# Emitting the next batch's attention in hand-ordered small units inside this batch's FFN, with column-tiled AV, two-bank scores, Silu and 128-token output tiles

## The chip, the cores and the metric

One core of a Trainium2 chip. The metric is the device time of one execution in microseconds (us), lower is better. Each kernel was run several times; runs of one kernel agree within about 1%, all runs quoted here are of the fast state (none lies more than 1.5% above the fastest of its kernel), and each experiment was timed beside the kernel before on the same chip.

Names of engines in the profile: PE is the matrix engine, PEld its weight loads, DVE the vector engine, ACT the scalar (activation) engine, POOL the engine that issues the cast-while-loading DMAs here, SP the one that issues the output DMAs. Both kernels put the sums of their matmuls into tiles of PSUM (the `psum` and `ps_` pools), from which DVE and ACT read them; a bank below is the part of such a tile that holds the scores of one head. The granted clock is the share of its full speed that the profile records for PE.

## The reference

Attention without softmax (squared relu; its second product, attention times V, is called AV below), then a gated FFN with an RMS norm. Eight batches of 448 tokens, 12 heads of 64, model width 768, FFN width 1536.

```python
scores = (1 / sqrt(64)) * q @ k.T                 # per batch and head, 448 x 448
attn   = maximum(scores, 0) ** 2 / 448
x      = concat_heads(attn @ v)                   # 3584 tokens x 768
xn     = x / sqrt(mean(x * x) + 1e-6) * rms_g
out    = (silu(xn @ w_gate) * (xn @ w_val)) @ w_out
```

Everything on PE is bf16 with fp32 sums.

## The kernel before

Tokens of a batch are cut into four chunks of 112 (`PC`). For a pair of heads, Q and K are transposed on PE, scores are computed per chunk and head (64-row matmuls, one PSUM bank each), relu is shared between ACT (head 0) and DVE (head 1), the square is on DVE. AV uses a zero-padded V, 128 columns wide, so that both heads of a pair add into one [128, 448] tile. `xT` is the transposed attention output, which the FFN of the same batch reads.

```python
def attention_pair(b, j, xT, qkv, fillers=()):
    ...                                            # transposes, copies to QT and KT_
    for c in range(NCH):
        for hh in range(2):
            psS = psum.tile([PC, S], FP32, tag=tg, bufs=bf)
            nc.tensor.matmul(out=psS[:], lhsT=KT_[prt, c*PC:(c+1)*PC], rhs=QT[prt, :], ...)
        rA: nc.scalar.activation(Relu, pss[0]);  nc.vector.tensor_tensor(rA * rA)
        rB: nc.vector.tensor_relu(pss[1]);       nc.vector.tensor_tensor(rB * rB)
    if fillers: fillers.pop(0)()                   # a piece of the FFN of batch b-1
    for hh in range(2):
        for c in range(NCH):
            nc.tensor.matmul(out=psAV[:], lhsT=vpad[:, c, hh, :], rhs=rsq[hh][c][:], ...)
    ...
    nc.scalar.mul(out=xT[:, j, :], in_=psAV[:], mul=inv_attn)

def norm():
    x2 = xT * xT                                   # one DVE instruction, 2688 columns
    for kt in range(KT): psSS += ones @ x2[:, kt]  # PE: sum over the model width
    rstdb = Sqrt(psSS / 768 + eps)                 # ACT
    nc.vector.reciprocal(rstdb)                    # DVE
    for kt in range(KT): xn[:, kt] = xT[:, kt] * g * rstdb      # DVE, six instructions

def gate(fb):                                      # 12 of these per batch
    psG = wg.T @ xn (6 matmuls);  psV = wv.T @ xn (6 matmuls)
    sig = Sigmoid(psG)                             # ACT
    t1 = sig * psG;  hT[:, fb, :] = t1 * psV       # DVE, two instructions

def outproj(u):                                    # four tiles of 112 tokens per batch
    for o, w in ((0, 512), (512, 256)):
        12 matmuls: psO += hT[:, fk, u*PC:(u+1)*PC].T @ wo_sb[:, fk, o:o+w]
        nc.vector.tensor_copy(ost[:, o:o+w], psO)

for b in range(NB):                                # FFN of batch b-1 as fillers in attention of b
    work = ffn_chunks(b - 1, ...)                  # [norm, gate x 12, outproj x 4]
    for j in range(HP): attention_pair(b, j, xT, qkvs[j], fillers=3 pieces of work)
ffn_batch(NB - 1, ...)
```

The norm of a batch is the *first* piece of its FFN, so it comes when the attention of that batch has just ended. The tile scheduler is free to reorder instructions.

## Time and profile before

| | before |
|---|---|
| device time, median | 645.35 us (643.21 to 646.93) |
| span of the profiled run | 641.8 us |
| first reciprocal (one per batch, in the norm) | 59.1 us |
| from reciprocal to reciprocal, batches 2 to 6 | 75.1 us each |
| from the last reciprocal to the end | 54.8 us |
| PE / DVE / ACT busy | 90% / 69% / 40% |

The one reciprocal of each batch is a good clock: the table above is the start, the period and the end. (The first period is longer, 83.8 us, and the last shorter, 68.6; the seven together are 527.9.) These lines are from the page of the profile: span, busy time of each engine with its share, then busy tenths in 40 slices of the span for PE and DVE, and the granted PE clock in tenths.

```profile
span 641.8 us, 8357 instructions
...
PE 575.7 (90%) x3120; PEld 292.4 (46%) x3120; DVE 445.1 (69%) x951; ACT 255.4 (40%) x498; POOL 116.4 (18%) x134
...
PE   5465999979999799988999799997999989997997
...
DVE  4745677578776778669775797857786697757452
...
PEclk9855899998999799997999989997999979998999
```

PE is near 9 everywhere after the start, and about every fifth slice has a dip in PE and in the clock. The timeline around one dip (start us, duration us, engine, line, operation; in brackets the idle time before it and what ended it; rows between are left out):

```profile
286.70 1.28 ACT L230 ACT_TABLE_LOAD   x1
...
286.74 0.59 PE L180 MATMUL psS<-QT,KT 64*112 64x448 bf16 x4 [0.30 <-ACT KT L167]
...
287.99 0.63 ACT L230 ACTIVATE rstdb<-psSS,eps_col 128x448 f32<-128x448 f32 x1
...
293.11 2.94 DVE L237 RECIPROCAL rstdb<-rstdb 128x448 f32<-128x448 f32 x1
...
296.22 3.05 DVE L240 SCALAR_TENSOR_TENSOR xn<-xT,g_sb,rstdb 128x448 bf16<-128x448 bf16 x5
...
296.94 0.57 PE L258 MATMUL psG<-xn,wg_sb 128*128 128x448 bf16 x1
```

From the Sqrt at 287.99 to the first gate matmul at 296.94 the FFN has nothing for PE. The reciprocal starts 4.5 us after Sqrt has ended, and DVE fills that time with relu and squares of the next attention. In the meantime PE has only scraps of attention. Two windows around it (from:to and length in us, then us busy and instructions of PE, PEld, DVE, ACT, POOL, then granted clock, DMA share, GB/s):

```profile
288.00:296.00 8.00, 5.70 (x25) 1.92 (x24) 6.91 (x13) 4.09 (x8) 0.00 (x0) 0.72 0.04 17
296.00:304.00 8.00, 7.53 (x32) 3.35 (x33) 7.97 (x18) 4.40 (x9) 1.40 (x2) 0.85 0.23 16
```

The clock is down to 0.72 and 0.85. And three of the costliest groups (line, engine, operation, output and inputs, shapes, count; busy us and mean ns; idle before):

```profile
L258 PE MATMUL psG<-xn,wg_sb 128*128 128x448 bf16 x576 | 151.1, 364 | 11.5 <-DVE xn L240 8.9
...
L291 PE MATMUL psO<-wo_sb,hT 128*112 128x512 bf16 (+1 forms) x768 | 136.2, 327 | 0.0
...
L200 PE MATMUL psAV<-rA,vpad 112*128 112x448 bf16 x192 | 61.0, 382 | 12.4 <-DMA vpad<-in_v_dram 10.0
```

The mean of 364 ns is not the pace of the matmuls, since the records of neighbouring ones overlap. The pace is better read from a dense stretch of the timeline: 12 gate and value matmuls in a row (from 302.55 us) take 2.27 us, 0.189 us each.

### The profile page before, as it was taken

What the parts mean: (1) busy time and instruction counts of PE and PEld (TensorE: products, weight loads), DVE (VectorE), ACT (ScalarE), POOL (GpSimd) and SP (SyncE); (2) the same over time, 40 slices, a digit from 0 to 9 for tenths busy, and PEclk for the clock granted to TensorE, in tenths of its full rate; (3) what the DMA queues carried; (4) which work ended last, traced back from release to release, by engine and by line L of the source; (5) the groups of instructions that cost most, each with busy time, mean ns of one, the idle gap of its engine ahead of it and who ended that gap; (6) DMA issues with size and microseconds to landing.
All of it is one profiled execution on the core that took longest, in us unless ns stands there. A gap on an engine that the chain in (4) does not pass through costs nothing. (4 is left out here: it accounts for less than half of the span.)

```text
span 641.8 us, 8357 instructions
## 1 busy us (share of the span) xinstructions
PE 575.7 (90%) x3120; PEld 292.4 (46%) x3120; DVE 445.1 (69%) x951; ACT 255.4 (40%) x498; POOL 116.4 (18%) x134
## 2 busy tenths in 40 slices
PE   5465999979999799988999799997999989997997
PEld 2121444644446344553445444463445534454455
DVE  4745677578776778669775797857786697757452
ACT  5532545244532544245352445425442354522210
POOL 9442311301014001130013010040001000100000
PEclk9855899998999799997999989997999979998999
DMA  9999922591119611391124912197112311211002
GB/s 74 169 204 188 125 14 16 69 118 13 11 8 117 77 8 9 37 157 8 7 16 61 126 9 15 7 111 83 8 9 37 72 8 9 14 44 43 1 2 86
DMA packets 139016, 35.14 MB, mean 55 GB/s; under 512 B 132320, under 2 KB 133856, under 8 KB 138976
## 3 DMA queue, kind: packets, MB, share of 16 engines
q0 software_dynamic: 134096, 23.60, 49.3%
q1 hardware_dynamic: 4880, 11.02, 5.5%
q8 instruction: 24, 0.39, 0.2%
q14 instruction: 16, 0.13, 0.1%
HBM read 47.19 MB, written 11.01 MB: 91 GB/s over the span
## 5 line engine op out<-in xcount | busy, mean ns | idle before, releaser
L258 PE MATMUL psG<-xn,wg_sb 128*128 128x448 bf16 x576 | 151.1, 364 | 11.5 <-DVE xn L240 8.9
L193 DVE TENSOR_SCALAR rB<-psS 112x448 bf16<-112x448 f32 x192 | 117.3, 616 | 36.6 <-PE psS L180 36.5
L267 PE MATMUL psV<-xn,wv_sb 128*128 128x448 bf16 x576 | 140.8, 360 | 0.8 <-DVE hT L278 0.2
L291 PE MATMUL psO<-wo_sb,hT 128*112 128x512 bf16 (+1 forms) x768 | 136.2, 327 | 0.0
L109 POOL DMA_DIRECT2D vpad<-in_v_dram x48 | 38.8, 809 | 404.7 <-PE psAV L200 156.9
L180 PE MATMUL psS<-QT,KT 64*112 64x448 bf16 x384 | 88.0, 404 | 24.0 <-ACT rA L189 10.8
L189 ACT ACTIVATE rA<-psS 112x448 bf16<-112x448 f32 x192 | 98.1, 542 | 26.4 <-PE psS L180 25.5
L291 PEld LDWEIGHTS <-hT 128*112 128x112 bf16 x768 | 90.4, 130 | 38.5 <-issue 7.0
L275 ACT ACTIVATE sig<-psG 128x448 bf16<-128x448 f32 x96 | 51.5, 543 | 111.2 <-PE psG L258 80.1
L190 DVE TENSOR_TENSOR rA<-rA 112x448 bf16<-112x448 bf16 x192 | 73.2, 381 | 22.0 <-ACT rA L189 21.5
L267 PEld LDWEIGHTS <-wv_sb 128*128 128x128 bf16 x576 | 54.5, 99 | 68.2 <-issue 27.1
L258 PEld LDWEIGHTS <-wg_sb 128*128 128x128 bf16 x576 | 55.1, 100 | 60.4 <-issue 22.4
L194 DVE TENSOR_TENSOR rB<-rB 112x448 bf16<-112x448 bf16 x192 | 73.4, 382 | 0.3
L200 PE MATMUL psAV<-rA,vpad 112*128 112x448 bf16 x192 | 61.0, 382 | 12.4 <-DMA vpad<-in_v_dram 10.0
L298 DVE COPY ost<-psO 112x512 f32<-112x512 f32 x64 | 35.5, 555 | 49.6 <-PE psO L291 49.6
L200 PEld LDWEIGHTS <-vpad 112*128 112x128 bf16 x384 | 36.7, 103 | 59.1 <-issue 26.4
L180 PEld LDWEIGHTS <-KT 64*112 64x112 bf16 x384 | 28.3, 132 | 77.6 <-issue 53.1
L167 ACT COPY QT<-psT 128x448 bf16<-128x448 bf16 x48 | 25.5, 531 | 90.4 <-PE psT L162 90.2
L200 PE MATMUL psAV<-rB,vpad 112*128 112x448 bf16 x192 | 56.7, 395 | 0.0
L209 ACT ACTIVATE xT<-psAV 128x448 bf16<-128x448 f32 x48 | 26.1, 544 | 68.6 <-PE psAV L200 68.6
L110 POOL DMA_DIRECT2D vpad<-in_v_dram x48 | 38.3, 798 | 0.2
L167 ACT COPY KT<-psT 128x448 bf16<-128x448 bf16 x48 | 25.5, 531 | 30.8 <-PE psT L162 30.7
(243 smaller groups left out, 389.3 us busy)
## 6 DMA issues: line engine op xcount, KB each, us to landing
out_dram<-ost SPq DMA_DIRECT2D x32, 336.0 KB, 2.7
vpad<-in_v_dram POOLq DMA_DIRECT2D x96, 56.0 KB, 2.8
qb<-in_q_dram POOLq DMA_DIRECT2D x7, 672.0 KB, 9.3
kb<-in_k_dram POOLq DMA_DIRECT2D x7, 672.0 KB, 12.4
wg_sb<-in_moe_w_gate_dram POOLq DMA_DIRECT2D x1, 2304.0 KB, 18.0
wv_sb<-in_moe_w_val_dram POOLq DMA_DIRECT2D x1, 2304.0 KB, 25.4
wo_sb<-in_moe_w_out_dram POOLq DMA_DIRECT2D x1, 2304.0 KB, 16.2
qp<-in_q_dram POOLq DMA_DIRECT2D x6, 112.0 KB, 5.1
```

The costliest lines, as they stand in the source:

```text
L109: nc.gpsimd.dma_start(out=vpad[:, :, 0, 0:D], in_=v_head_ap(b, 2 * j))
L167: nc.scalar.copy(out=dst[:], in_=psT[:, ti, :])
L180: nc.tensor.matmul(out=psS[:], lhsT=KT_[prt, c * PC : (c + 1) * PC], rhs=QT[prt, :], start=True, stop=True,)
L189: nc.scalar.activation(out=rA[:], in_=pss[0][:], func=ACT.Relu)
L190: nc.vector.tensor_tensor(out=rA[:], in0=rA[:], in1=rA[:], op=ALU.mult)
L193: nc.vector.tensor_relu(out=rB[:], in_=pss[1][:])
L194: nc.vector.tensor_tensor(out=rB[:], in0=rB[:], in1=rB[:], op=ALU.mult)
L200: nc.tensor.matmul(out=psAV[:], lhsT=vpad[:, c, hh, :], rhs=rsq[hh][c][:], start=(hh == 0 and c == 0), stop=(hh == 1 and c == NCH - 1),)
L258: nc.tensor.matmul(out=psG[:], lhsT=wg_sb[:, kt, fb * P : (fb + 1) * P], rhs=xn[:, kt, :], start=(kt == 0), stop=(kt == KT - 1),)
L267: nc.tensor.matmul(out=psV[:], lhsT=wv_sb[:, kt, fb * P : (fb + 1) * P], rhs=xn[:, kt, :], start=(kt == 0), stop=(kt == KT - 1),)
L275: nc.scalar.activation(out=sig[:], in_=psG[:], func=ACT.Sigmoid)
L291: nc.tensor.matmul(out=psO[:, :w], lhsT=hT[:, fk, u * PC : (u + 1) * PC], rhs=wo_sb[:, fk, o : o + w], start=(fk == 0), stop=(fk == FT - 1),)
```

## The change

The intent is to keep PE fed. The kernel declares a manual schedule, so each engine runs instructions in the order in which the program emits them. That order is built by `merge`: gate, value and out-projection units of batch b, with small units of the attention of b+1 spread over the first 90% of them, the norm of b+1 the last of these. In detail: AV writes each head of a pair to its own 64 columns (no zero padding); two heads' scores lie in two neighbouring banks, so relu and square take 896 columns per instruction (three quarters of the relu on ACT); Silu replaces Sigmoid and a multiply; the out-projection works on 128-token tiles over two batches, seven in place of eight; q, k and v are loaded in 512-byte pieces (in the kernel before, most packets of the trace have 128 bytes) and reordered on DVE; weights are loaded in slices. Some copies out of PSUM also change engine: that of the transposed Q and K goes from ACT to DVE, that of the output from DVE to ACT.

```diff
+def merge(main, side, head=0.0, tail=0.0):
+    total = sum(c for c, _ in main)
+    ...
+    for c, f in main:
+        while k < n and done >= total * (head + (1.0 - head - tail) * k / n):
+            out.append(side[k][1]); k += 1
+        out.append(f); done += c
+    ...
+    ctx.enter_context(tc.manual_schedule())
...
-                psS = psum.tile([PC, S], FP32, name="psS", tag=tg, bufs=bf)
+            psS = ps_s.tile([PC, 2, 512], FP32, name="psS", tag="psS")
...
-            nc.scalar.activation(out=rA[:], in_=pss[0][:], func=ACT.Relu)
-            nc.vector.tensor_relu(out=rB[:], in_=pss[1][:])
+            if on_dve:                                   # every fourth
+                nc.vector.tensor_relu(out=r[:], in_=psS[:, :, :S])
+            else:
+                nc.scalar.activation(out=r[:], in_=psS[:, :, :S], func=ACT.Relu)
+            nc.vector.tensor_tensor(out=r[:], in0=r[:], in1=r[:], op=ALU.mult)
...
-                    out=psAV[:],
-                    lhsT=vpad[:, c, hh, :],
+                    out=psAV[hh * D : (hh + 1) * D, :],
+                    lhsT=ld["v", b][:, 2 * j + hh, c * D : (c + 1) * D],
...
-            nc.scalar.activation(out=sig[:], in_=psG[:], func=ACT.Sigmoid)
-            nc.vector.tensor_tensor(out=t1[:], in0=sig[:], in1=psG[:], op=ALU.mult)
+        nc.scalar.activation(out=s[:], in_=psG[:], func=ACT.Silu)
...
+    def attention(b):
+        units = [(0.4, lambda: transposes(b, 0))]
+        for j in range(HP):
+            units.append((0.5, lambda j=j: scores(b, j, (0, 1))))
+            if j + 1 < HP:
+                units.append((0.4, lambda j=j: transposes(b, j + 1)))
+            units.append((0.5, lambda j=j: scores(b, j, (2, 3))))
+            if j:
+                units.append((0.8, lambda j=j: attend(b, j - 1)))
+        units.append((0.8, lambda: attend(b, HP - 1)))
+        return units
...
+    for fn in merge([], attention(0) + [(1.1, lambda: norm(0))]):
+        fn()
+    for b in range(B):
+        if b + 1 < B:
+            side = attention(b + 1) + [(1.1, lambda b=b: norm(b + 1))]
+        ...                                              # loads of batch b + 2
+        for fn in merge(ffn(b), side, 0.0, 0.1):
+            fn()
```

## The prediction

> **What bounds the kernel now.** PE. Page: PE 90% busy, DVE 69%, ACT 40%. The reciprocal of each batch's norm (timeline) marks the period: 142.9, 218.0, 293.1 ... 518.4 us, 75.1 us per batch. The first comes at 59.1 us (PE waits 9.4 us for a vpad DMA); 54.8 us follow the last.
>
> Dense streams run at full speed: 12 gate/value matmuls take 2.27 us (189 ns for 448 columns), 24 out-projection matmuls 3.94 us. Score pairs (64 rows) already run concurrently: four take 0.58 us. PE work per batch at that pace: gate/value 27.2, out-projection 15.8, scores about 8, AV 48 x 0.189 = 9.1, transposes 3, norm 1.3, together 64-65 us. The other 10 us come around the norm: from 286.7 to 296 us PE runs only bits of attention, waiting for Sqrt, reciprocal (2.94 us) and xn (6 x 0.6 us), and the clock drops to 0.72-0.85 (about 3.4 us lost).
>
> **What the change does to PE, per batch (estimates from these durations).**
> - AV in two 64-column tiles: 24 slots of 0.189[...]: 6 us in place of about 10.[...]
> - 128-token tiles: 7 tiles per two batches in place of 8: 13.8 us in place of 15.8.
> - Scores in fours: about 0.61 us x 12 = 7.3. Transposes 3.3, gate/value and norm as before.
> Sum: even batches 57 us, odd 61.
>
> **Norm.** It is now issued with 5.1 us of out-projection behind it. Chain after its sum: Sqrt 0.63, reciprocal 2.94, xn 3.7, then two reorder copies before the next transposes: about 8 us. So PE idles about 3 us at each boundary, some clock loss (1.5 us mean), and about 1.5 us of small waits: period 62 (even), 66 (odd).
>
> **Other engines.** DVE per batch: squares 24 x 0.61 = 14.8, relu 6 x 1.08 = 6.5, psT copy about 4, reorder 3.4, hT 7.4, norm 6.6, x2 2.3: about 45 us, 72% of the period. ACT: relu 18 x 0.92 = 16.6, Silu 6.5, xT 3.3, copies 3.5, norm with two table loads 3.2: 33 us. Neither becomes the limit. Silu saves one DVE multiply (12 x 0.62).
>
> **Start.** Attention of batch 0 runs alone and is DVE-bound: about 6 us per pair, 36 us, beginning near 7 us; first reciprocal near 47 us in place of 59[...].
>
> **Sum.** First matmul of FFN 0 near 51; four even periods of 62 and three odd of 66: 446; clock and start losses 4; last FFN 43 plus 4.5 tail and its bubble: 50. Span about 551; the timed run is 4.5 us above the span (646.3 against 641.8). **Predicted 556 us, 80% range 533 to 592.** Faster by over 2%: 0.97; within 2%: 0.02; slower: 0.01.
>
> **What would show it.** Reciprocals 62-66 us apart; AV pairs starting together (eight matmuls in about 0.75 us); PE idle 2-4 us before each batch's first gate matmul, released by xn or the reorder copies; clock mean above 0.94; first reciprocal at 45-50 us; DVE 65-75%.
>
> **What would make it wrong.** Column tiles not running together (+4.5 us per batch, about +36); the strict order letting ACT or DVE bursts stall PE inside the FFN (+3 us per batch is +21); the boundary gap throttling the clock every time (+2 us each)..

What is cut is marked. In the AV item the 6 us are 24 x 0.189 = 4.5 us plus 1.5 us, and the sums of 57 and 61, 551 and 556 us hold it. Measured afterwards, a group of eight took 0.88 us, 0.12 more than 4 x 0.189. Of the loads the pages show this: the POOL queue moved 23.6 MB before and after, in 134096 and in 40560 packets, whose time was 49.3% and 31.7% of 16 engines' span.

That score pairs run concurrently is seen in the kernel before: four matmuls start at 286.735, .738, .968 and .972 us. The 3.4 us of lost clock are worked out from the two windows above (8 x 0.28 + 8 x 0.15). The 1.5 us of clock and 1.5 us of small waits per period, and the durations of forms that the kernel before does not have, were estimates. Measured in the changed kernel are 0.916 us for a relu of 896 columns on ACT and 1.084 on DVE, 0.625 for a square of 896, 0.620 for the copy of psT and 0.29 for a reorder copy.

## The result and the profile after

| | before | after |
|---|---|---|
| device time, median | 645.35 us | 548.32 us (546.71 to 548.87) |
| ratio | | 0.850 (0.848 to 0.853) |
| span of the profiled run | 641.8 | 544.9 |
| first reciprocal | 59.1 | 43.95 |
| the seven periods together | 527.9 | 447.2 |
| one even / odd period, late in the run | 75.1 / 75.1 | 61.7 / 64.3 |
| last reciprocal to the end | 54.8 | 53.8 |

Even and odd count the batch whose FFN fills the period; an even one has three token tiles, an odd one four.

A ratio is the mean time of one kernel's fast runs over that of the kernel before in the same rounds, so it is not quite the ratio of the medians that are quoted. Of the 96.9 us of span that went away, the periods gave 80.7, the start 15.2 and the end 1.0. The profiled run is the fastest of its four, 1.6 us under the median. The same lines of the page as before:

```profile
span 544.9 us, 7394 instructions
...
PE 485.1 (89%) x3024; PEld 236.1 (43%) x3024; DVE 338.6 (62%) x586; ACT 252.3 (46%) x369; POOL 34.4 (6%) x45
...
PE   3774999879999799888999799987999899989996
...
DVE  3886677467764677566774677656775677745210
...
PEclk9976999979999899999999999999999999999999
```

PE's share has not risen (90% to 89%); its work became less, and its dips are narrower. From the third boundary on the clock stays at full speed. That is a part of the gain too: in the seven periods and the last FFN PE was busy at half clock for 39.3 us before and 9.5 us after. Gate and value matmuls of the changed kernel started 0.373 us apart at half clock (116.0 to 120.1 us) and 0.189 at full, so half of these times was lost, and about 15 us of the gain is clock (an estimate from the clock records of the two traces). The timeline around one boundary, which answers to the one shown of before:

```profile
231.97 0.95 PE L207 MATMUL psAV<-r,vb 112*64 112x448 bf16 x8
...
232.85 2.76 PE L286 MATMUL psO<-wo_sb,hT 128*128 128x512 bf16 x12
...
236.43 1.48 PE L238 MATMUL psSS<-x_1924,ones_bf 128*128 128x448 bf16 x6
...
237.75 5.37 PE L286 MATMUL psO<-wo_sb,hT 128*128 128x256 bf16 x36
...
239.06 2.95 DVE L246 RECIPROCAL rstd<-rstd 128x448 f32<-128x448 f32 x1 [1.55 <-ACT rstd L243]
...
242.05 3.67 DVE L249 SCALAR_TENSOR_TENSOR xn<-xT,g_sb,rstd 128x448 bf16<-128x448 bf16 x6
...
245.63 0.29 DVE L148 COPY qp<-qb 112x512 bf16<-112x512 bf16 x1
...
245.97 0.37 PE L163 MATMUL psT<-ident,qp 112*128 112x112 bf16 x4 [2.85 <-DVE qp L148]
```

The norm's sum on PE (236.43) is followed by 36 out-projection matmuls, which cover Sqrt, the reciprocal and the first part of xn. PE then waits 2.85 us for the reorder copy of the next batch's Q. The first two rows are one AV group: eight matmuls, from 231.97 until the next unit at 232.85, 0.88 us. The same groups as before:

```profile
L260 PE MATMUL psG<-xn,wg_sb 128*128 128x448 bf16 x576 | 129.4, 360 | 1.1 <-DVE xn L249 1.0
...
L286 PE MATMUL psO<-wo_sb,hT 128*128 128x512 bf16 (+1 forms) x672 | 115.2, 326 | 0.0
...
L207 PE MATMUL psAV<-r,vb 112*64 112x448 bf16 x384 | 47.7, 370 | 4.6 <-DVE qkT L169 3.8
```

And what PE itself waited for (total us, times, longest):

```profile
engine line waited for: us in total, times, longest us
PE psT L163 <- DVE qp L148: 29.6, 8, 7.6
PE psS L182 <- ACT r L197: 7.4, 11, 1.0
```

The first of these holds the boundary: eight waits, 29.6 us. The timeline has them as 4.84 us for the very first load, 7.6 us between the first norm and the first FFN, and 2.86 us at six later boundaries. The reorder copy comes last in a chain of Sqrt, reciprocal and xn, so the copy is named but the chain is what is waited for.

### The profile page after: what moved, and what is told of

It is laid out like the page before. It is cut to its first block, busy times and chain, and to the rows that moved or that the text cites. A ratio compares the mean times of both kernels' runs of the same rounds, so it can differ in the third digit from the quotient of the medians.

```text
span 544.9 us, 7394 instructions
## 1 busy us (share of the span) xinstructions
PE 485.1 (89%) x3024; PEld 236.1 (43%) x3024; DVE 338.6 (62%) x586; ACT 252.3 (46%) x369; POOL 34.4 (6%) x45
## 3 DMA queue, kind: packets, MB, share of 16 engines
q0 software_dynamic: 40560, 23.60, 31.7%
## 4 chain that ended last, share of the span: by engine, by line
PE 73%; DVE 14%; ACT 8%; issue 2%; DMA 1%; POOL 0%; ACTq 0%; POOLq 0%
PE psV L260 20%; PE psG L260 20%; PE psO L286 14%; PE psAV L207 8%; PE psS L182 8%; DVE xn L249 5%; DVE rstd L246 4%; ACT r L197 4%; PE psT L163 3%; ACT L243 2%; DVE r L198 2%; DVE r L195 1%; ACT rstd L243 1%; DMA kb<-in_k_dram 1%; ACT xT L215 1%
## 5 line engine op out<-in xcount | busy, mean ns | idle before, releaser
L198 DVE TENSOR_TENSOR r<-r 112x896 bf16<-112x896 bf16 x192 | 119.3, 625 | 93.8 <-ACT r L197 91.9
L197 ACT ACTIVATE r<-psS 112x896 bf16<-112x896 f32 x144 | 127.0, 916 | 52.5 <-PE psS L182 52.4
L286 PE MATMUL psO<-wo_sb,hT 128*128 128x512 bf16 (+1 forms) x672 | 115.2, 326 | 0.0
L271 ACT ACTIVATE sil<-psG 128x448 bf16<-128x448 f32 x96 | 52.3, 545 | 102.2 <-PE psG L260 90.8
L277 DVE TENSOR_TENSOR hT<-sil,psV 128x448 bf16<-128x448 bf16 x96 | 59.4, 618 | 45.9 <-PE psV L260 37.8
L286 PEld LDWEIGHTS <-hT 128*128 128x128 bf16 x672 | 63.6, 98 | 49.2 <-issue 9.3
L182 PE MATMUL psS<-qkT 64*112 64x448 bf16 x384 | 64.5, 394 | 19.3 <-ACT r L197 7.4
L260 PEld LDWEIGHTS <-wg_sb 128*128 128x128 bf16 x576 | 53.0, 99 | 59.8 <-issue 19.2
L260 PEld LDWEIGHTS <-wv_sb 128*128 128x128 bf16 x576 | 52.3, 99 | 57.5 <-issue 19.2
L195 DVE TENSOR_SCALAR r<-psS 112x896 bf16<-112x896 f32 x48 | 52.0, 1084 | 0.0
L207 PE MATMUL psAV<-r,vb 112*64 112x448 bf16 x384 | 47.7, 370 | 4.6 <-DVE qkT L169 3.8
L163 PE MATMUL psT<-ident,qp 112*128 112x112 bf16 x192 | 19.0, 226 | 29.6 <-DVE qp L148 29.6
L207 PEld LDWEIGHTS <-vb 112*64 112x64 bf16 x384 | 19.1, 111 | 28.9 <-issue 21.4
L246 DVE RECIPROCAL rstd<-rstd 128x448 f32<-128x448 f32 x8 | 23.6, 2953 | 12.8 <-ACT rstd L243 12.8
L169 DVE COPY qkT<-psT 128x896 bf16<-128x896 bf16 x48 | 29.8, 620 | 2.3 <-PE psT L163 2.1
```

The costliest lines, as they stand in the source:

```text
L163: nc.tensor.transpose(out=psT[:, ti, c * PC : (c + 1) * PC], in_=ldp[nm, b, j][:, c, :, :], identity=ident[:],)
L182: nc.tensor.matmul(out=psS[:, hh, :S], lhsT=t[prt, 1, c * PC : (c + 1) * PC], rhs=t[prt, 0, :], start=True, stop=True,)
L195: nc.vector.tensor_relu(out=r[:], in_=psS[:, :, :S])
L197: nc.scalar.activation(out=r[:], in_=psS[:, :, :S], func=ACT.Relu)
L198: nc.vector.tensor_tensor(out=r[:], in0=r[:], in1=r[:], op=ALU.mult)
L207: nc.tensor.matmul(out=psAV[hh * D : (hh + 1) * D, :], lhsT=ld["v", b][:, 2 * j + hh, c * D : (c + 1) * D], rhs=rsq[b, j, c][:, hh, :], st ...
```

## The experiments

Two accounts were set against each other. **Theory A**: the periods are the length of PE's own stream plus its waits around the norm; the gain is less PE work (AV, token tiles) and a better covered norm. **Rival B**: the gain came from relieving DVE, whose busy time fell from 445 to 339 us. A third account was not tested by a run: the changed loads. In the first 60 us of the kernel before PE waits 16.2 us for DMAs (vpad 10.0, qp 5.3, kp 0.9), after that only 1.0 us; so the loads may explain much of the 15.2 us at the start, and can explain next to nothing of the later periods. Each experiment starts from the changed kernel unless it says otherwise; differences are to its 548.3 us.

| run | edit | median us | difference |
|---|---|---|---|
| x1_av_serial | AV head by head | 549.4 | +1.1 |
| x2_tiles112 | 112-token tiles | 559.5 | +11.2 |
| x3_norm_last | norm after the FFN | 592.5 | +44.1 |
| x4_sigmoid | Sigmoid and a multiply | 548.5 | +0.2 |
| x8_av_full128 | AV weights 128 wide (wrong result) | 578.1 | +29.8 |
| x9_av_split | heads of a pair apart | 596.0 | +47.7 |
| x5_tail20 | side units over 80% | 526.2 | -22.1 |
| x6_auto | no manual schedule | 511.9 | -36.5 |
| x7_onebank | relu and square per bank | 558.1 | +9.8 |
| y1_auto_tail20 | x6 and x5 together | 507.0 | -41.3 |
| y2_auto_startact | x6, first relus all on ACT | 512.2 | -36.1 |
| b2_coltile | kernel before with column-tiled AV only | 644.1 | -1.3 to before |

The changed kernel was not run again in these batches; the kernel before was, with medians of 644.77, 645.52 and 645.37 us in the three batches, beside 645.35 in the first runs.

### x4_sigmoid: does DVE time count?

```diff
-        nc.scalar.activation(out=s[:], in_=psG[:], func=ACT.Silu)
-        sil[b, fb] = s
+        nc.scalar.activation(out=s[:], in_=psG[:], func=ACT.Sigmoid)
+        nc.vector.tensor_tensor(out=t1[:], in0=s[:], in1=psG[:], op=ALU.mult)
+        sil[b, fb] = t1
```

> The changed kernel with Sigmoid and the extra DVE multiply of before (96 of 0.62 us, 60 us of DVE work, 62% to about 72% of the span). Theory A: 0 to +6 us. Rival B: +35 to +60 us.

Measured: 548.5 us, ratio 0.851 (0.849 to 0.853). The engine line of its page:

```profile
PE 487.4 (89%) x3024; PEld 237.0 (43%) x3024; DVE 390.4 (71%) x682; ACT 252.4 (46%) x369; POOL 34.4 (6%) x45
```

DVE works 390.4 us in place of 338.6 and nothing gets slower. Rival B falls, as far as it is about the sum of DVE's work; the added work stands inside the FFN, so the 4.5 us by which the kernel before kept its reciprocal waiting are not tested here. Silu is a free tidy-up in this kernel and no measurable part of the gain.

### x2_tiles112: the token tiles

```diff
-        for t in range(full) if b % 2 == 0 else range(full, NT):
+        for t in range((b % 2) * NCH, (b % 2) * NCH + NCH):
-   lhsT=hTs[i][:, fk, t * P : (t + 1) * P]
+   lhsT=hTs[i][:, fk, t * PC : (t + 1) * PC]      # copies and stores cut to 112 in the same way
```

> The changed kernel with 112-token out-projection tiles, four in each batch, as before the change. Theory A: one tile (3.9 us of PE) more in each of the four even batches, +15.7 us, less about 1.4 us per even period where two score groups now stand back to back and the fourth tile would part them: +10 to +16 us. Rival B: under +4 us.

Measured: 559.5 us, +11.2, ratio 0.868 (0.865 to 0.871). The seven periods grew from 447.2 to 457.8 us, and the even ones now are as long as the odd ones (64.4 us late in the run). Inside the range of theory A.

### x3_norm_last: where the norm stands

```diff
-            side = attention(b + 1) + [(1.1, lambda b=b: norm(b + 1))]
+            side = attention(b + 1) + [(0.0, lambda: None)]
         for fn in merge(ffn(b), side, 0.0, 0.1):
             fn()
+        if b + 1 < B:
+            norm(b + 1)
```

> The changed kernel, but the norm of the next batch is issued after the last out-projection unit and not with three units (5.1 us) behind it; nothing else moves. Theory A: PE's wait at each of seven boundaries grows from 2.9 to about 8 us, and the granted clock drops each time (2 to 3 us more): +45 to +60 us. Rival B: DVE's work and order hardly change, under +20 us.

Measured: 592.5 us, +44.1, a hair below the range; ratio 0.919 (0.917 to 0.921). Of PE's waits:

```profile
PE psT L163 <- DVE qp L148: 61.5, 8, 8.2
```

Without the two at the start (4.9 and 7.6 us) these are six waits of 8.2 us in place of 2.86, and at every boundary one window of 8 us has a clock of only 0.64 to 0.69. Late periods are 68.8 and 71.1 us in place of 61.7 and 64.3: 7 us each, of which 5.3 are the wait; the rest, about 1.7, is put down to the clock (an estimate by subtraction). Of the parts that were undone here, the position of the norm costs the most.

### x1_av_serial, x8_av_full128, x9_av_split: the column tiles

The first try to take the tiles apart was to swap the loops:

```diff
-        for c in range(NCH):
-            for hh in range(2):
+        for hh in range(2):
+            for c in range(NCH):
```

> The changed kernel, but the AV loop runs head by head, so that two neighbouring matmuls always use the same 64 columns of the array[...]; work, data and result stay the same. Theory A (the periods are the length of PE's own stream): 24 more slots of 0.189 us per batch, 4.5 us in each of the seven full periods, little at the start where DVE sets the pace: +30 to +34 us, about 580 us, ratio to before about 0.90. Rival B (the gain came from relieving DVE, busy 339 us in place of 445; PE has slack): under +8 us.

That matmuls of one head would not overlap was the assumption; x9 below measured 0.88 us for four of them.

Measured: 549.4 us, +1.1, ratio 0.851 (0.845 to 0.856): no effect. Taken alone this looks like evidence against the column tiles. The trace says otherwise; one AV group and the unit after it:

```profile
233.24 0.96 PE L207 MATMUL psAV<-r,vb 112*64 112x448 bf16 x8
234.13 2.76 PE L286 MATMUL psO<-wo_sb,hT 128*128 128x512 bf16 x12
```

Eight matmuls still take 0.89 us, and their records start in pairs 13 to 14 ns apart, 0.19 to 0.21 us from pair to pair. The experiment had not removed what it meant to remove. Two further runs did. The first makes the weights 128 columns wide, with numbers that are wrong on purpose:

```diff
-                    out=psAV[hh * D : (hh + 1) * D, :],
-                    lhsT=ld["v", b][:, 2 * j + hh, c * D : (c + 1) * D],
+                    out=psAV[:],
+                    lhsT=ld["v", b][:, 2 * j + hh, min(c, 2) * D : (min(c, 2) + 2) * D],   # start and stop to match
```

> Wrong result on purpose. The changed kernel with AV weights 128 columns wide (two neighbouring chunks of one head, so the numbers are wrong), eight matmuls into one accumulation, as many and as wide as before the change; nothing else moves. The run before this one (head by head) did not slow down, and its trace shows pairs still starting together. If column tiles are still what made AV shorter, each group of eight takes 8 x 0.189 and not 4 x 0.189 us, 0.75 us more, 4.5 us per period: +30 to +34 us. If a narrow or a wide weight makes no difference: under +5 us.

Measured: 578.1 us, +29.8 (just under the range), ratio 0.896 (0.894 to 0.898). The group and the unit after it:

```profile
245.42 1.68 PE L207 MATMUL psAV<-r,vb 112*128 112x448 bf16 x8
246.94 2.76 PE L286 MATMUL psO<-wo_sb,hT 128*128 128x512 bf16 x12
```

The group takes 1.52 us in place of 0.88; eight times 0.189 is 1.51. In the profiled spans 23.7 us of the loss lie in the seven periods, 3.4 us each, and 8.7 us at the start, which is more than the scatter of the starts (see x7_onebank) and was not traced. The second puts the two heads into different units with other work between them:

```diff
+            def s23(j=j):
+                if j:
+                    attend_head(b, j - 1, 0)       # four matmuls of head 0
+                scores(b, j, (2, 3))
...
-                units.append((0.8, lambda j=j: attend(b, j - 1)))   # both heads
+                units.append((0.8, lambda j=j: attend(b, j - 1)))   # head 1 only
```

> The changed kernel, but in five of six head pairs the four AV matmuls of head 0 are issued before the second score group and those of head 1 in the place of before, with out-projection or gate work between, so the two column tiles are never waiting together. Theory C[...]: four matmuls of one head now take 4 x 0.189 us alone, 0.75 us more for a pair, +27 to +36 us in all[...]. Theory D (a 64-column matmul simply takes half of the time of a 128-column one, alone too): 0 to +8 us.

Theory C comes down to this: the two heads' matmuls overlap only when they stand in one group.

Measured: 596.0 us, +47.7, above the range of theory C and far from D; ratio 0.924 (0.921 to 0.927). Four matmuls of one head, and the unit after them:

```profile
310.53 0.94 PE L210 MATMUL psAV<-r,vb 112*64 112x448 bf16 x4
311.41 1.31 PE L277 MATMUL psV<-xn,wv_sb 128*128 128x448 bf16 x6
```

One head alone takes 0.88 us for four matmuls, as long as both heads together. So theory D is out: in these traces a narrow matmul is not faster by itself (0.22 us each), and only the eight of both heads in one group come to 0.11 us each. The part beyond the range came at the start: the first reciprocal moved from 44 to 60 us, while the seven periods grew by 32.6 us, within it.

With x9, each pair of x1 is most likely one matmul of each head, although four of head 0 stand in front of the first of head 1 in the program: four of one head alone take 0.88 us, and the eight of x1 took 0.89. The records do not name the head, so this is an inference from these two times; it was not shown.

### x7_onebank: relu over two banks

```diff
-            nc.scalar.activation(out=r[:], in_=psS[:, :, :S], func=ACT.Relu)   # and DVE, and square
+            for hh in range(2):
+                nc.scalar.activation(out=r[:, hh, :], in_=psS[:, hh, :S], func=ACT.Relu)
```

> The changed kernel with relu and square done per head on one PSUM bank (448 columns), as before, in place of two heads at once (896). ACT gets about 3 us and DVE about 4.4 us more per batch (the fixed cost of twice as many instructions); PE's work stays. Theory A (PE's stream sets the periods): 0 to +8 us, most of it at the start. Rival B (DVE and ACT time is what counts): +30 us or more.

The cost of more instructions is seen in the two kernels: 448 and 896 columns take 0.542 and 0.916 us for the relu on ACT, 0.616 and 1.084 for that on DVE, 0.382 and 0.625 for the square, so 896 take less than twice as long.

Measured: 558.1 us, +9.8, a little over the range of theory A, and not mostly at the start as expected; ratio 0.864 (0.862 to 0.867). The periods grew by 8.3 us (63.6 and 66.4 us late in the run). The start is 4 us later, but kernels with an unchanged start already differ by 2.5 us there (43.95 to 46.4 us), and x1_av_serial, which is no slower, has 48.2, so that part is not resolved. DVE goes from 339 to 370 us, less than in x4_sigmoid, where nothing got slower. What differs is that relu stands on PE's way: scores reuse two PSUM buffers, and a later release is a wait. The wait of the scores for ACT, 7.4 us in the changed kernel, here:

```profile
PE psS L182 <- ACT r L198: 11.4, 15, 1.1
```

That accounts for at most 4 us. More goes through the clock. Two stretches of one boundary, the second right after the first (columns as in the windows above):

```profile
246.71:250.12 3.41, 0.97 (x11) 0.71 (x12) 3.35 (x9) 0.00 (x0) 0.00 (x0) 1.00 0.56 171
250.13:253.54 3.41, 3.41 (x10) 1.16 (x8) 0.25 (x1) 1.83 (x2) 0.00 (x0) 0.50 0.00 0
```

The wait at the boundary is 2.86 us as in the changed kernel, but here half clock follows it at all six boundaries (3.4 us of it at five, 6.8 at the sixth), there only at the first two (6.8 and 3.4 us). PE is busy at half clock for 22.5 us in place of 9.5, which costs about 6.5 us (an estimate from these two times). All four runs agree with it: their mean granted clock is 0.96, that of the changed kernel's runs 0.97 to 0.99.

Why the same wait of 2.86 us was followed by half clock at six boundaries of one kernel and at two of the other was not shown: no run moved a wait alone.

### b2_coltile: the column tiles without the rest

The kernel before, with only this:

```diff
-        for hh in range(2):
-            for c in range(NCH):
-                    out=psAV[:],            lhsT=vpad[:, c, hh, :],
+        for c in range(NCH):
+            for hh in range(2):
+                    out=psAV[hh * D : (hh + 1) * D, :],
+                    lhsT=vpad[:, c, hh, hh * D : (hh + 1) * D],   # start and stop to match
```

> The kernel before with one thing of the change: AV in two 64-column tiles, chunk by chunk, everything else (its own order of work, zero-padded V tiles) as it was. If the saving of 0.75 us per group of eight arrives there too: 6 groups x 0.75 = 4.5 us per batch, -25 to -36 us. If its scheduler mixes AV matmuls with others one by one, the tiles meet less often and the norm gap stays: -5 to -25 us.

Measured: 644.1 us, ratio 0.998 (0.995 to 1.001): nothing, outside both ranges. The timeline of PE points to why:

```profile
315.78 0.38 PE L200 MATMUL psAV<-rA,vpad 112*64 112x448 bf16 x1
316.09 0.36 PE L258 MATMUL psG<-xn,wg_sb 128*128 128x448 bf16 x1
316.38 0.38 PE L200 MATMUL psAV<-rB,vpad 112*64 112x448 bf16 x1
316.38 0.38 PE L200 MATMUL psAV<-rA,vpad 112*64 112x448 bf16 x1
316.69 0.36 PE L258 MATMUL psG<-xn,wg_sb 128*128 128x448 bf16 x1
```

The scheduler puts gate and score matmuls between the AV matmuls. From the start of a lone AV matmul to the next unit it is 0.31 us (315.78 to 316.09), where a dense 128-column matmul takes 0.189; a pair takes 0.31 us as well (316.38 to 316.69), where two dense ones take 0.378; and the gate matmul between them takes 0.29. So in these lines a lone AV matmul and the gate matmul after it take 0.12 and 0.10 us more than a dense matmul, and there are many such short groups: from 143 to 518 us the 240 AV matmuls stand in 115 groups, 55 of them of one matmul. In the changed kernel AV comes one head pair later, as a group of eight, and there the tiles are worth 30 us. In the old order that part of the change is worth nothing. That the grouping alone makes the difference is argued from these two traces; no run added it to the kernel before.

### x5_tail20, x6_auto, y1_auto_tail20, y2_auto_startact: what the new order still loses

```diff
-        for fn in merge(ffn(b), side, 0.0, 0.1):
+        for fn in merge(ffn(b), side, 0.0, 0.2):
```

> The changed kernel with the side units spread over the first 80% of each FFN and not 90%, so that the norm is issued with 9.0 us of out-projection behind it and not 5.1. Theory A: the wait of 2.86 us at each of six or seven boundaries goes (the chain is 8.0 us long), and so does the clock drop of the first boundaries; denser side units cost up to 1.5 us of waits per period: -10 to -22 us, about 530 us.

Measured: 526.2 us, -22.1, a hair beyond the range; ratio 0.816 (0.814 to 0.817). PE's first wait of 29.6 us:

```profile
PE psT L163 <- DVE qp L148: 12.5, 2, 7.6
```

Only the two at the start are left; late periods are 58.2 and 62.6 us. The six waits that went were 17.1 us, and the half clock after the first two of them cost about 4.8, together the 22.1 within 0.2 us.

```diff
-    ctx.enter_context(tc.manual_schedule())
```

> The changed kernel without the declaration of a manual schedule: the scheduler may reorder what the program emits. Theory A with grouping (order matters: groups of one array mode are broken up, the norm moves): +15 to +60 us. If the scheduler keeps the emitted order where nothing waits: within 5 us.

Measured: 511.9 us, -36.5, ratio 0.794 (0.791 to 0.797). Both branches of the expectation were wrong: the units as emitted are a good *source*, and strict obedience to their order costs time. Two of PE's waits, 29.6 and 7.4 us in the changed kernel:

```profile
PE psT L162 <- DVE qp L147: 5.0, 1, 5.0
...
PE psS L181 <- ACT r L196: 1.8, 7, 0.6
```

And a boundary, on PE:

```profile
283.02 5.26 PE L285 MATMUL psO<-wo_sb,hT 128*128 128x256 bf16 x35
288.12 0.36 PE L162 MATMUL psT<-ident,qp 112*128 112x112 bf16 x4
288.31 0.36 PE L162 MATMUL psT<-ident,kp 112*128 112x112 bf16 x4
288.51 0.35 PE L259 MATMUL psG<-xn,wg_sb 128*128 128x448 bf16 x1
288.70 0.35 PE L259 MATMUL psV<-xn,wv_sb 128*128 128x448 bf16 x1
```

The transposes of the next batch follow the out-projection without a wait, since nothing puts their reorder copies behind xn, and then gate and value matmuls alternate, so that each part of xn feeds two matmuls when it arrives. Late periods are 56.9 and 60.65 us, which are the 57 and 61 us that the prediction summed for PE's own work.

```diff
-    ctx.enter_context(tc.manual_schedule())
-        for fn in merge(ffn(b), side, 0.0, 0.1):
+        for fn in merge(ffn(b), side, 0.0, 0.2):
```

> The changed kernel with both: scheduler free to reorder, and side units spread over 80%. If the free scheduler has already taken all waits out of the full periods (they are 56.9 and 60.65 us there, the sums of PE's own work), within 3 us of the free scheduler alone (512 us); otherwise 3 to 10 us faster.

Measured: 507.0 us, -41.3, ratio 0.786 (0.784 to 0.787), correct: the best version, 7.5% under the changed kernel. It is 4.9 us under x6, the second branch of its expectation; the even periods stay at 56.9 us, and the gain lies mostly in the first period (53.6 us for 57.7) and in about 1 us of each odd one; the end is 1.3 us longer. The engine line of its page, 95% for PE:

```profile
PE 480.8 (95%) x3024; PEld 234.7 (47%) x3024; DVE 331.0 (66%) x586; ACT 251.7 (50%) x369; POOL 34.3 (7%) x45
```

```diff
-    ctx.enter_context(tc.manual_schedule())
-            on_dve = state["n"] % 4 == 3
+            on_dve = b > 0 and state["n"] % 4 == 3
```

> The changed kernel with the scheduler free, and all relu of the first batch's attention on ACT (DVE loses 6 x 1.08 us there). If that start is bound by DVE, as the prediction said: -4 to -7 us against 512. If it is a chain through PE, ACT and DVE with none of them full: within 2 us, or slower.

Measured: 512.2 us, ratio 0.793 (0.791 to 0.795), within 0.4 us of x6_auto. Taking about 6.5 us of relu off DVE in the first attention does not help, with the free scheduler; in strict order it was not tried. So the start is not bound by DVE; from 4 to 44 us of the changed kernel DVE was busy 28.9 us of 40. A chain through PE, ACT and DVE would fit, but no run shows it. What would shorten it stays open.

## Why the prediction was right, and where not

The predicted time, 556 us, and its range hold the measured 548.3. Point by point:

- *PE bounds the kernel, AV and tiles make its work shorter.* Shown. AV: 0.88 us per group against 1.52 (x8), so 3.8 us per batch, as the "6 us in place of about 10" said; worth 29.8 us in all, the start included. Tiles: 11.2 us (x2). PE's own sums of 57 and 61 us were met when the waits were taken out (x6: 56.9 and 60.65).
- *The norm covered by 5.1 us of out-projection, PE idle about 3 us at each boundary.* Shown: 2.86 us, released by the reorder copy, and undoing the position costs 44 us (x3).
- *DVE and ACT are not the limit; Silu saves only DVE time.* Shown for Silu by x4. For the relus it is too simple: x7 costs 9.8 us with DVE at 66%, at most 4 us of it because scores wait for their buffers, about 6.5 by the clock.
- *Clock and sum.* The sum was about 8 us high, mostly in the clock. I put 1.5 us of clock loss into every period, and 4 us more for clock and start; the first two boundaries lost about 4.8 us together and the later ones nothing; in x7 the same wait was followed by half clock at all six, and why is not shown. In the terms of the sum: the start to the first gate matmul was predicted 51 and measured 51.6 us, the stretch to the first gate matmul of the last FFN 446 + 4 and measured 443.4, the end 50 and measured 49.9. Each run was 1.8 us over its span and not 4.5; the median is another 1.6 us over the profiled run. A slip partly hid the size of the clock term: 57 and 61 us with the three extras of 3, 1.5 and 1.5 are 63 and 67, not the 62 and 66 that were summed. What a late even period consists of is 56.9 us of work (x6), 2.86 of the boundary and about 1.9 of small waits: 61.7.
- *Start bound by DVE, about 36 us.* The time came out near (first reciprocal 43.95, predicted 47), the reason did not: y2 shows that less DVE work does not shorten the time, and DVE was busy for 28.9 of 40 us.
- *Strict order may stall PE* stood in the list of risks at 3 us per batch. It was the larger truth about this change: the strict order costs 36.5 us against the scheduler on the very same units (x6), and still 19.2 us when the norm has its longer cover (x5 against y1). I never asked whether the units or their fixed order bring the gain.

Undoing the parts one at a time gives 44.1 (norm position), 29.8 (AV width), 11.2 (tiles), 9.8 (two banks) and 0.2 (Silu), together 95.1 us, beside the 97.0 that the change brought. That they nearly add up is partly chance: none of them undoes the loads, though the start gave 15.2 us, the norm of before was not placed like that of x3, x7's cost is largely clock, and b2 shows that the parts depend on each other.

## What to carry to other kernels

Find the instruction that happens once per period, and read start, period and end from it; then sum the work of the bounding engine per period and call the rest waits. Put the long serial chain of a stage (here sum, Sqrt, reciprocal, scale) as far ahead of its use as there is independent work to cover it: 9 us of cover was right for a chain of 8, 5 us was not. Cut work into units that keep narrow matmuls together (here the gain was 29.8 us in groups of eight and nothing in short groups, x8 and b2), but test whether a fixed order is better than a scheduler that starts from the same units. An experiment that shows no effect has to be checked in the trace for having removed its cause.
